# VectorE's small operations behind the following maximum, reciprocals taken from the sums in place, and a third tile's ranks as sums of signs by ScalarE

## The chip, the cores and the metric

The kernel runs on one core of a Trainium2 chip. The core has a matrix engine (TensorE, PE in the profile; its weight loads are PEld), VectorE (DVE), ScalarE (ACT), GpSimd (POOL), SyncE (SP, which here only issues DMAs), and DMA queues. The engines run their own instruction streams and meet through semaphores. The metric is device time of one execution in microseconds. An operation on an engine starts before the one ahead of it has fully ended, so in a timeline two durations overlap a little; the distance from start to start is what an operation costs its engine, and it is given where it matters.

## The reference

Two blocks, one behind the other.

```python
# attention: B, H, S, D = 8, 8, 576, 64
scores = q @ k^T / sqrt(D)
kth    = 32nd largest score of each row
attn   = softmax(where(scores >= kth, scores, -1e9))   # sum + 1e-9 in the divisor
x      = (attn @ v) as (B, S, H*D = 512)
# mixture of depths, for each batch
gate   = x @ w_gate                                    # 576 numbers
idx    = the 128 rows with the largest gate
out    = x;  out[idx] += sigmoid(gate[idx]) * (relu(x[idx] @ w1) @ w2)
```

Every one of 8 x 8 x 576 rows needs its 32nd largest score, and each batch needs the ranks of its 576 gates.

## The kernel before, in words

**Units.** A tile is 128 query rows of a batch; a batch has five tiles t = 0 to 4 (the last one, J, has 64 rows). A unit is one tile for two heads (for the last tile, four heads packed into 128 rows), so a batch has 18 units and the kernel 144. The loop `for n in range(-1, N)` (line 1192) is a software pipeline, written out by hand: the helper class `InOrder` (line 38) keeps each engine's instructions in program order, and since it records every operation, all of them carry line 46 in the profile. Nothing is planned by costs; the order in the code is the order on each engine.

**One step n of the pipeline.**

- VectorE does `bound_of(n)` (line 1143, `find_bound` at line 544): seven MAX8 over parts of each of two score rows (14 in all, `cand<-sc`), then rounds of MAX8 and MATCH_REPLACE8 on the candidates, which end in `bound`, a bound near the row's 24th largest score. After that `kth_of(n - 2)` takes two MAX8 over 584 elements (`next<-y`), whose eighth value is the wanted 32nd largest score of unit n - 2.
- ScalarE takes the exponentials of unit n - 4 (`pT`, `last`), the signs of scores against the bound of unit n - 1 with their sum (`sides`, `seen`), one mask of unit n - 3 (`less`), copies of transposed keys or queries (`kT`, `qT`), the scores of unit n + 1 out of PSUM (`sc`), and the weighted values (`xs`).
- GpSimd makes the other mask of unit n - 3 (`less`, line 603), then whatever is queued in `vector_late` for it and in `pool_late`, then `y = sc * sides` for both rows of unit n - 1 and a small fill of eight columns (`weigh_signs`, line 1160).
- TensorE turns (transposes) and masks unit n - 4, multiplies scores of unit n + 1, and multiplies by the values.

**Lists of delayed work.** `late` and `copies_late` are run by ScalarE just ahead of the next `sc` copy, `vector_late` by VectorE between the two halves of the 14 maxima (line 552), `amid_late` among the second seven, `pool_late` by GpSimd at line 1308, `kept` right behind the values, and `after_kth` behind `kth_of`.

**The end of a tile.** When a tile's last values are in `xs` (128 x 8 x 65, of which the 65th column is the sum of the weights), `keep_sums` (line 735) copies the eight sums to `sums` on ScalarE, adding 1e-9. In the next step `normalise` (line 730) takes their reciprocal on VectorE (`rden`) and multiplies on GpSimd (`x<-xs,rden`). One step later, `gates` runs `dot` (line 1028) on VectorE: the product of `x` and `wg` with its sum, the operation `prod<-x,wg`, which reads two tensors from SBUF.

**The mixture of a batch** (line 786) is a generator which the loop advances at the steps in `mix_at` (line 1072) while the next batch's units run. Its first pieces find ranks: for tiles 0 and 1, `weigh_gates` (line 839) lets ScalarE sum the signs of the differences of one gate and all gates, writing the signs themselves over the tile `pick`; for tiles 2, 3 and 4, `choose` (line 861) lets VectorE count larger gates (`junk<-gate_row,gate`, 576 elements, and an accumulator read). `choose_slot` (line 823) then compares the rank with slot numbers on GpSimd (`pick`). It is queued for both tiles 0 and 1 behind the signs of tile 1. With the usual `mix_at`, the sign of tile 0 runs at unit 8 of a batch's 18, and the two picks of tiles 0 and 1 at unit 10. Later, `add_up` (line 895) makes `place`, `row_i` and `g` on VectorE, one behind the other; `squash` (line 906) adds 1 to `g` and inverts it; `keep_least` (line 1174) reduces the 36 values of a batch's last `next`.

Of the kernel before, what the change touches and what calls it, by code (L numbers as in the profile page):

```python
# [10 lines left out]
AF = mybir.ActivationFunctionType  # L11
# [17 lines left out]
FEWEST = 0.5  # L29
# [3 lines left out]
J = 4  # L33
# [16 lines left out]
def kernel(  # L50
# [91 lines left out]
    seen = const.tile([P, NS], FP32, name="seen")  # L142
    least = const.tile([P, B], FP32, name="least")
    bounded = const.tile([P, NS], FP32, name="bounded")
    sums = const.tile([P, B * NT, H], FP32, name="sums")
    nc.gpsimd.memset(sums, 1.0)

    MIDDLE = S - 2 * (TOP_K - 8) + 1
    steps_i = const.tile([P, 2, 8], I32, name="steps_i")
# [8 lines left out]
    nc.gpsimd.memset(ranks, 0.0)  # L158


    signs = const.tile([P, B - 1, 2], FP32, name="signs")
    places = const.tile([P, B, 7], FP32, name="places")
    nc.gpsimd.memset(places, 1.0)
    slot_signs = const.tile([P, CAP], FP32, name="slot_signs")
# [59 lines left out]

    kept, values_bank = [], [None]

    after_kth = []

    def flush_copies():
        while copies_late:  # L230
# [14 lines left out]

    def flush_all():
        flush_vector()
        flush()
        flush_pool()

# [293 lines left out]
    def find_bound(sc, bound):  # L544

        cand = wkpool.tile([P, 2, 8 * PARTS], FP32, name="cand")
        best = [stats.tile([P, 2, 8], FP32, name=f"best{r}") for r in range(2)]
        best.append(bound)
        for i in range(2):

            if i == 1:
                flush_vector()
            for u in range(PARTS):
                if i == 1 and amid_late and u == amid_late[0][0]:
                    amid_late.pop()[1]()
                dve.max(
                    cand[:, i, 8 * u : 8 * u + 8],
                    sc[:, i, u * S // PARTS : (u + 1) * S // PARTS],
                )


        parts = cand.rearrange("p i (u e) -> p i u e", u=PARTS)
# [151 lines left out]
    def keep_values_of_two(t, g, av, xs):  # L714
# [7 lines left out]
        for i, (h, r) in enumerate(heads_of(t, g)[0]):  # L722
# [4 lines left out]
                in_=both[r : r + n, :].rearrange("p (g c) -> p g c", g=2),  # L727
            )

    def normalise(b, t, xs):  # L730
        n = R if t == J else P
        den = sums[0:n, b * NT + t, :]
        divide(n, xs, of_batch[b][0][0:n, t, :], den)

    def keep_sums(n, xs, den):
        act.activation(den, xs[0:n, :, D], AF.Copy, bias=1e-9)

    def divide(n, xs, x, den):
        rden = stats.tile([P, H], FP32, name="rden")
        dve.reciprocal(out=rden[0:n, :], in_=den)  # L740
        pool.tensor_tensor(
            x.rearrange("p (h d) -> p h d", h=H),
            xs[0:n, :, 0:D],
            rden[0:n, :].unsqueeze(2).to_broadcast([n, H, D]),
            ALU.mult,
        )

# [38 lines left out]
    def mixture(row0, pg, rank, exact=False, sign_sum=None):  # L786
# [47 lines left out]
        for t in range(NT):  # L834
            yield
            n = R if t == J else P


            def weigh_gates(t=t):
                total = sign_sum[:, t : t + 1]  # L840
                act.activation(
                    pick.rearrange("p t c -> p (t c)")[:, 0:S],
                    gate_row,
                    AF.Sign,
                    bias=gate[:, t : t + 1],
                    scale=-1.0,
                    accum_out=total,
                )
                if t == 1:
                    for u in range(2):  # L850
                        pool_late.append(
                            lambda u=u: choose_slot(
                                u, P, slot_signs, sign_sum[:, u : u + 1]
                            )
                        )

            if t < 2 and not exact:
                late.append(weigh_gates)
                continue

# [33 lines left out]

        def add_up():
            add_parts(place, found)
            keep_rows(
                place,
                row_i,
                row0 if isinstance(row0, float) else row0[:, 0:1],  # L900
                float(done * S - 1),
            )
            dve.tensor_scalar_max(out=g, in0=place[:, 1:2], scalar1=-88.0)
            late.append(lambda: act.activation(g, g, AF.Exp, scale=-1.0))

        def squash():
            dve.tensor_scalar_add(out=g, in0=g, scalar1=1.0)
            dve.reciprocal(out=g, in_=g)

        kept.append(lambda: after_kth.append(add_up))  # L910
        if exact:
            for todo in (kept, after_kth):
                while todo:
                    todo.pop(0)()
        yield
# [258 lines left out]
    def keep_least(b, bound, kth):  # L1174
        at = 2 * per_batch * b
        late.append(
            lambda: act.copy(
                out=bounded[:, at : at + 2 * per_batch].rearrange("p (n i) -> p n i", i=2),
                in_=bound,
            )  # L1180
        )
        dve.tensor_reduce(
            out=least[:, b : b + 1], in_=kth, axis=mybir.AxisListType.XY, op=ALU.min
        )

    def mask_of(n, on=None):
# [5 lines left out]
    for n in range(-1, N):  # L1192
# [89 lines left out]
        if is_unit(n - 4):  # L1282
            b4, t4, g4 = units[n - 4]
            values(t4, g4, pT, last, av, qkv[b4][2], 2 * DE * second)
            if n in place_steps:
                values_bank[0] = av
                next(mixtures[place_steps[n]])
                pieces[place_steps[n]] += 1
            if g4 == 0:
                xs = xpool.tile([P, H, DE], FP32, name="xs")  # L1290
                if t4 == 0:
                    x = xpool.tile([P, NT, HD], FP32, name="x")
                    pg = gates_of[b4 % 2]
                    of_batch[b4] = x, pg
            if second:
                keep_values_of_two(t4, g4 - 1, av, xs)
            if g4 == groups(t4) - 1:
                inverting = b4, t4, xs
                n4 = R if t4 == J else P
                keep_sums(n4, xs, sums[0:n4, b4 * NT + t4, :])  # L1300
            while kept:
                kept.pop(0)()

# [64 lines left out]
        b, t, g = units[m]  # L1368
        keep_values(t, g, weighed[m][3], xs)

    def sums_of(t, xs):
        n = R if t == J else P
        keep_sums(n, xs, sums[0:n, (B - 1) * NT + t, :])
# [76 lines left out]
    dve.tensor_tensor(  # L1450
        x[0:R, J, :].rearrange("p (h d) -> p h d", h=H),
        xs[0:R, :, 0:D],
        rden[0:R, :].unsqueeze(2).to_broadcast([R, H, D]),
        ALU.mult,
    )
    store_last(last_out, x)
# [77 lines left out]
        )  # L1534

    keep_least(B - 1, bounds.pop(B - 1)[:, :, :, 7], next8s.pop(B - 1)[:, :, :, 7])
    flush()
    low = modpool.tile([P, S], I32, name="low", tag="scratch")[:, 0:NS]
    dve.tensor_scalar(
# [9 lines left out]
    for what, op, than, limit in (  # L1549
# [5 lines left out]
        (sums.rearrange("p t h -> p (t h)"), ALU.min, ALU.is_gt, FEWEST),  # L1555
        (sums.rearrange("p t h -> p (t h)"), ALU.max, ALU.is_lt, MOST),
        (places[:, :, 6], ALU.min, ALU.is_gt, 0.5),
        (places[:, :, 6], ALU.max, ALU.is_lt, 1.5),
    ):
# [68 lines left out]
    def general_weights(sc):  # L1628

        p = wkpool.tile([P, 2, S], FP32, name="p", tag="y")  # L1630
        for i in range(2):
# [10 lines left out]
            e = wkpool.tile([P, S], FP32, name="e", tag="sides")  # L1642
            nc.scalar.activation(
                e, sc[:, i, :], AF.Exp, bias=shift, scale=scale
            )
# [10 lines left out]
    def general(b, row0):  # L1656
# [11 lines left out]
        for t in range(NT):  # L1668
# [14 lines left out]
            den = stats.tile([P, H], FP32, name="den", bufs=1)  # L1683
            keep_sums(rows, xs, den[0:rows, :])
            divide(rows, xs, x[0:rows, t, :], den[0:rows, :])
# [46 lines left out]
```

## Time and profile before

| what | value |
|---|---|
| median of 3 runs | 787.77 us (785.72 to 788.05) |
| the profiled execution's own time | 788.09 us |
| its span on the core | 785.8 us |
| VectorE busy, whole span | 755.1 us (96%) |
| ScalarE busy | 731.7 us (93%) |
| TensorE matmul busy | 725.5 us (92%) |
| GpSimd busy | 693.7 us (88%) |
| VectorE busy from 40 to 740 us | 699.20 of 700 us |
| ScalarE busy from 40 to 740 us | 688.49 of 700 us |

The span is the time on the core that the profile covers; what lies around it is 788.09 - 785.8 = 2.3 us. A row of the profile's groups gives engine, operation, what is written and read with shapes, the count, busy time and mean duration of one, then the idle time of the engine ahead of these operations and what ended it. A row of a timeline gives the start in us from the span's start, the duration in us, engine, line, operation, and in brackets idle time ahead of it.

### The profile page before, as it was taken

To read this page: it belongs to the slowest core of one execution; us is meant where nothing else is said; L and a number is where in the kernel's file an instruction comes from. 1 tells how busy PE (TensorE), PEld (TensorE's weight loads), DVE (VectorE), ACT (ScalarE), POOL (GpSimd) and SP (SyncE) were. 2 spreads that over 40 slices of the span, in tenths; PEclk is the share of its full clock that TensorE was granted. 3 is DMA by queue.
4 is the path that set the end of the run, shared out by engine and by line. 5 is a ranking of instruction groups with operands and counts; after the bars stand their busy time and mean duration, and the time that the engine had idled before them with its cause. 6 is when DMAs were issued, how large, how long until landed. Compare 5 with 4: busy or idle time off the path is not lost. (4 is left out here: it accounts for less than half of the span.)

```text
span 785.8 us, 33176 instructions
## 1 busy us (share of the span) xinstructions
PE 725.5 (92%) x12535; PEld 550.6 (70%) x12535; DVE 755.1 (96%) x4602; ACT 731.7 (93%) x1535; POOL 693.7 (88%) x732
## 2 busy tenths in 40 slices
PE   8888888788999989999999999999899999999987
PEld 6666666566786668766787667866687668757756
DVE  6999999999999999999999999999999999999952
ACT  5999999999999999999999999999999999989830
POOL 3899999999999999999999999999999999899821
PEclk9999999999999999999999999999999999999999
DMA  9941214121151223321232221412234102101021
GB/s 171 297 86 35 58 62 104 36 56 30 62 113 25 52 66 76 83 55 37 77 89 52 56 43 62 105 30 56 43 89 92 30 15 70 25 15 17 3 75 31
DMA packets 121751, 50.69 MB, mean 65 GB/s; under 512 B 116016, under 2 KB 116016, under 8 KB 120560
## 3 DMA queue, kind: packets, MB, share of 16 engines
q1 hardware_dynamic: 118368, 43.94, 22.9%
q0 software_dynamic: 1744, 4.20, 3.0%
q8 instruction: 101, 1.65, 0.9%
q14 instruction: 66, 0.54, 0.3%
q10 hardware_dynamic: 1472, 0.36, 0.2%
HBM read 36.93 MB, written 11.55 MB: 62 GB/s over the span
## 5 line engine op out<-in xcount | busy, mean ns | idle before, releaser
L46 POOL TENSOR_TENSOR y<-sc,sides 128x576 f32<-128x576 f32 x288 | 350.5, 1240 | 27.9 <-ACT sides L46 26.2
L46 DVE MAX8 cand<-sc 128x8 f32<-128x82 f32 (+1 forms) x2016 | 312.8, 228 | 4.6 <-ACT sc L46 4.6
L46 POOL TENSOR_SCALAR less<-sc,next 128x576 bf16<-128x576 f32 x135 | 233.7, 1731 | 24.6 <-DVE next L46 21.9
L46 ACT ACTIVATE sides<-sc,bound 128x576 fp8e4<-128x576 f32 x288 | 230.9, 802 | 2.1 <-DVE bound L46 1.5
L46 PEld LDWEIGHTS av<-v,pT 128*64 128x64 f32 x4608 | 146.9, 138 | 87.5 <-ACT last L46 79.0
L46 DVE MAX8 next<-y 128x8 f32<-128x584 f32 x288 | 204.4, 751 | 0.0
L46 PE MATMUL av<-v,pT 128*64 128x65 f32 x4608 | 166.9, 225 | 35.2 <-ACT last L46 34.9
L46 PE MATMUL ps<-kT,qT 64*128 64x288 f32 (+1 forms) x1248 | 170.4, 422 | 3.2 <-ACT sc L46 2.5
L46 PEld LDWEIGHTS <-less 64*128 64x128 bf16 (+1 forms) x2448 | 160.6, 131 | 11.2 <-POOL less L46 8.3
L46 ACT COPY sc<-ps 128x1152 f32<-128x1152 f32 x140 | 160.7, 1148 | 0.0
L46 PE MATMUL ptr<-ident,sc 64*128 64x64 f32 x2272 | 160.1, 252 | 0.0
L46 ACT ACTIVATE pT<-ptr 128x1024 f32<-128x1024 f32 x142 | 147.4, 1038 | 9.4 <-PE ptr L46 8.7
L46 PEld LDWEIGHTS ptr<-ident,sc 64*128 64x128 f32 x2272 | 137.6, 137 | 23.8 <-issue 23.6
L46 PE MATMUL ptr<-out_of_reach,less 64*128 64x64 bf16 x2272 | 147.1, 189 | 5.6 <-POOL less L46 4.9
L46 ACT ACTIVATE less<-sc,next 128x576 bf16<-128x576 f32 x147 | 115.5, 790 | 0.0
L46 PEld LDWEIGHTS ps<-kT,qT 64*128 64x128 f32 (+1 forms) x1248 | 92.6, 176 | 22.8 <-ACT sc L46 5.6
L46 DVE MATCH_REPLACE8 cand<-best,cand 128x21 f32<-128x21 f32 (+1 forms) x576 | 99.0, 180 | 0.0
L46 DVE MAX8 best<-cand 128x8 f32<-128x21 f32 (+1 forms) x576 | 90.6, 190 | 0.0
L46 ACT ACTIVATION_READ_ACCUMULATOR sides<-sc,bound 128x1 f32 x288 | 63.8, 222 | 0.0
L46 PE MATMUL h_ps<-xeT,w 128*128 128x128 f32 x464 | 61.9, 278 | 0.0
L46 PEld LDWEIGHTS av<-ident,sc 128*128 128x128 f32 x144 | 20.0, 139 | 55.9 <-issue 40.9
L46 PE MATMUL av<-vpair,last 128*64 128x130 f32 x576 | 56.9, 276 | 0.0
(167 smaller groups left out, 919.0 us busy)
## 6 DMA issues: line engine op xcount, KB each, us to landing
v<-in_v_dram SPq DMA_DIRECT2D x64, 128.0 KB, 4.0
out_dram<-x SPq DMA_DIRECT2D x8, 1024.0 KB, 3.9
rows<-in_k_dram SPq DMA_DIRECT2D x56, 128.0 KB, 3.0
rows<-in_q_dram SPq DMA_DIRECT2D x56, 128.0 KB, 3.0
w<-in_moe_w_dram SPq DMA_DIRECT2D x2, 2048.0 KB
gate_row<-row_dram SPq DMA_DIRECT2D x7, 288.0 KB, 4.4
last<-in_q_dram SPq DMA_DIRECT2D x8, 128.0 KB, 3.4
vpair<-in_v_dram SPq DMA_DIRECT2D x16, 64.0 KB, 5.1
```

Of the source, the lines that this page charges most:

```text
L46: return lambda *a, **kw: self._tc.keep_in_program_order(fn(*a, **kw))
```

## The change

Four edits.

1. A new list `after_max`, emptied by `flush_small` behind each of the 14 maxima of `find_bound`. The reduction of `keep_least`, the operations of `add_up` behind `place` (now `use_place`), and the reciprocal of `squash` go into it.
2. `keep_sums` is gone. `invert` takes the reciprocal from the column of `xs` itself and keeps it in `shares`, from which GpSimd multiplies; `rden` and the addition of 1e-9 are gone. The final checks look at `shares` instead of `sums`.
3. The ranks of tile 2 come from `weigh_gates` on ScalarE as well (`SIGNED = 3`), and not from `choose` on VectorE.
4. The signs go to a tile of their own (`gate_signs`, fp8) and no longer over `pick`, and each tile's `choose_slot` is queued right behind its signs, so the pick of tile 0 now runs at unit 8 and no longer at unit 10.

The fallback for uncertain inputs (`general`) is changed in the same way and isn't run with these inputs.

```diff
-    sums = const.tile([P, B * NT, H], FP32, name="sums")
-    nc.gpsimd.memset(sums, 1.0)
+    shares = const.tile([P, B * NT, H], FP32, name="shares")
+    nc.gpsimd.memset(shares, 1.0)
...
-    signs = const.tile([P, B - 1, 2], FP32, name="signs")
+    SIGNED = 3
+    signs = const.tile([P, B - 1, SIGNED], FP32, name="signs")
...
-    after_kth = []
+    after_kth, after_max = [], []
+
+    def flush_small():
+        while after_max:
+            after_max.pop(0)()
...
                     sc[:, i, u * S // PARTS : (u + 1) * S // PARTS],
                 )
+                flush_small()
...
+    def share_of(b, t):
+        return shares[0 : R if t == J else P, b * NT + t, :]
+
     def normalise(b, t, xs):
         n = R if t == J else P
-        den = sums[0:n, b * NT + t, :]
-        divide(n, xs, of_batch[b][0][0:n, t, :], den)
-
-    def keep_sums(n, xs, den):
-        act.activation(den, xs[0:n, :, D], AF.Copy, bias=1e-9)
-
-    def divide(n, xs, x, den):
-        rden = stats.tile([P, H], FP32, name="rden")
-        dve.reciprocal(out=rden[0:n, :], in_=den)
+        invert(xs[0:n, :, D], share_of(b, t))
+        divide(n, xs, of_batch[b][0][0:n, t, :], share_of(b, t))
+
+    def invert(den, share):
+        dve.reciprocal(out=share, in_=den)
+
+    def divide(n, xs, x, share):
         pool.tensor_tensor(
             x.rearrange("p (h d) -> p h d", h=H),
             xs[0:n, :, 0:D],
-            rden[0:n, :].unsqueeze(2).to_broadcast([n, H, D]),
+            share.unsqueeze(2).to_broadcast([n, H, D]),
             ALU.mult,
         )
...
                 total = sign_sum[:, t : t + 1]
+                unread = modpool.tile([P, S], FP8, name="gate_signs")
                 act.activation(
-                    pick.rearrange("p t c -> p (t c)")[:, 0:S],
+                    unread,
                     gate_row,
                     AF.Sign,
                     bias=gate[:, t : t + 1],
                     scale=-1.0,
                     accum_out=total,
+                    saturate=False,
                 )
-                if t == 1:
-                    for u in range(2):
-                        pool_late.append(
-                            lambda u=u: choose_slot(
-                                u, P, slot_signs, sign_sum[:, u : u + 1]
-                            )
-                        )
-
-            if t < 2 and not exact:
+                pool_late.append(lambda: choose_slot(t, P, slot_signs, total))
+
+            if t < SIGNED and not exact:
                 late.append(weigh_gates)
                 continue
...
         def add_up():
             add_parts(place, found)
+            after_max.append(use_place)
+
+        def use_place():
             keep_rows(
...
         def squash():
             dve.tensor_scalar_add(out=g, in0=g, scalar1=1.0)
-            dve.reciprocal(out=g, in_=g)
+            after_max.append(lambda: dve.reciprocal(out=g, in_=g))
...
-        dve.tensor_reduce(
-            out=least[:, b : b + 1], in_=kth, axis=mybir.AxisListType.XY, op=ALU.min
+        after_max.append(
+            lambda: dve.tensor_reduce(
+                out=least[:, b : b + 1], in_=kth, axis=mybir.AxisListType.XY, op=ALU.min
+            )
         )
...
-                keep_sums(n4, xs, sums[0:n4, b4 * NT + t4, :])
...
-    sums_of(J - 1, xs)
...
-    sums_of(J, xs)
     count(J - 1, slice(0, JP), rank)
-    rden = stats.tile([P, H], FP32, name="rden")
-    dve.reciprocal(out=rden[0:R, :], in_=sums[0:R, (B - 1) * NT + J, :])
+    invert(xs[0:R, :, D], share_of(B - 1, J))
```

More of the change, by code (lines that the diff above doesn't have):

```diff
@@ L559, in find_bound @@
                 )
+                flush_small()
         parts = cand.rearrange("p i (u e) -> p i u e", u=PARTS)
@@ L907, in squash @@
             dve.tensor_scalar_add(out=g, in0=g, scalar1=1.0)
-            dve.reciprocal(out=g, in_=g)
+            after_max.append(lambda: dve.reciprocal(out=g, in_=g))
         kept.append(lambda: after_kth.append(add_up))
         if exact:
-            for todo in (kept, after_kth):
+            for todo in (kept, after_kth, after_max):
                 while todo:
@@ L1298 @@
                 inverting = b4, t4, xs
-                n4 = R if t4 == J else P
-                keep_sums(n4, xs, sums[0:n4, b4 * NT + t4, :])
             while kept:
@@ L1369, in keep_unit @@
         keep_values(t, g, weighed[m][3], xs)
-    def sums_of(t, xs):
-        n = R if t == J else P
-        keep_sums(n, xs, sums[0:n, (B - 1) * NT + t, :])
     def mask_both(m):
@@ L1452 @@
         xs[0:R, :, 0:D],
-        rden[0:R, :].unsqueeze(2).to_broadcast([R, H, D]),
+        share_of(B - 1, J).unsqueeze(2).to_broadcast([R, H, D]),
         ALU.mult,
@@ L1536 @@
     keep_least(B - 1, bounds.pop(B - 1)[:, :, :, 7], next8s.pop(B - 1)[:, :, :, 7])
+    flush_small()
     flush()
@@ L1554 @@
         (seen, ALU.min, ALU.is_gt, float(MIDDLE - 16)),
-        (sums.rearrange("p t h -> p (t h)"), ALU.min, ALU.is_gt, FEWEST),
-        (sums.rearrange("p t h -> p (t h)"), ALU.max, ALU.is_lt, MOST),
+        (shares.rearrange("p t h -> p (t h)"), ALU.max, ALU.is_lt, 1.0 / FEWEST),
+        (shares.rearrange("p t h -> p (t h)"), ALU.min, ALU.is_gt, 1.0 / MOST),
         (places[:, :, 6], ALU.min, ALU.is_gt, 0.5),
@@ L1641, in general_weights @@
             nc.vector.tensor_scalar_mul(shift, tops[0][:, 0:1], -scale)
-            e = wkpool.tile([P, S], FP32, name="e", tag="sides")
+            e = modpool.tile([P, S], FP32, name="e", tag="scratch")
             nc.scalar.activation(
@@ L1682, in general @@
             rows = R if t == J else P
-            den = stats.tile([P, H], FP32, name="den", bufs=1)
-            keep_sums(rows, xs, den[0:rows, :])
-            divide(rows, xs, x[0:rows, t, :], den[0:rows, :])
+            den = stats.tile([P, H], FP32, name="den", bufs=1)[0:rows, :]
+            act.activation(den, xs[0:rows, :, D], AF.Copy, bias=1e-9)
+            invert(den, den)
+            divide(rows, xs, x[0:rows, t, :], den)
             dot_tile(t, x, pg)
```

## The prediction

> **What bounds the kernel now.** I read the page's busy times first, then who waited for whom on VectorE, then the busy times by stretch, to see whether the 96% is an average over unlike stages.
>
> ```profile
> PE 725.5 (92%) x12535; PEld 550.6 (70%) x12535; DVE 755.1 (96%) x4602; ACT 731.7 (93%) x1535; POOL 693.7 (88%) x732
> ...
> 40.00:740.00 700.00, 654.82 (x11733) 496.70 (x11729) 699.20 (x4307) 688.49 (x1437) 658.28 (x665) 1.00 0.24 56
> 740.00:785.80 45.80, 35.99 (x384) 26.89 (x380) 23.58 (x85) 13.27 (x35) 12.39 (x18) 0.95 0.17 46
> ```
>
> The columns are length, PE, PEld, DVE, ACT, POOL, clock, DMA share, GB/s. From 40 to 740 us VectorE idles 0.8 us of 700; its waits lie at the two ends. So in the steady part a unit lasts as long as VectorE's instructions: a bare unit has 4.74 us from start to start, one with a count 5.47 us. What VectorE is spared there is gained, as long as ScalarE (688.49 of 700) and GpSimd keep their lead. The rows concerned:
>
> ```profile
> L46 DVE CUSTOM_DVE_ANT_0 prod<-x,wg 128x512 f32<-128x512 f32 x32 | 25.4, 794 | 0.1
> L46 DVE TENSOR_SCALAR_CACHE_REDUCE junk<-gate_row,gate 128x576 f32<-128x576 f32 x14 | 11.1, 793 | 0.0
> L46 ACT ACTIVATE sums<-xs 128x8 f32<-128x8 f32 x32 | 6.9, 216 | 1.0
> L46 DVE RECIPROCAL rden<-sums 128x8 f32<-128x8 f32 x32 | 5.9, 185 | 1.4 <-ACT sums L46 1.4
> ```
>
> **The skill.** The Trainium skill, "VectorE: DVE Perf Modes", section "The DRAIN you can't avoid", says that a semaphore between two VectorE operations costs nothing beyond the drain. The trace disagrees for these short ones:
>
> ```profile
> 380.42 1.42 DVE L46 MAX8 next<-y 128x8 f32<-128x584 f32 x2
> 381.88 0.22 DVE L46 TENSOR_REDUCE least<-next 128x1 f32<-128x36 f32 x1
> ...
> 366.62 0.14 DVE L46 TENSOR_REDUCE place<-places 128x2 f32<-128x6 f32 x1
> 366.80 0.15 DVE L46 TENSOR_SCALAR row_i<-place 128x1 int32<-128x1 f32 x1
> 366.87 0.14 DVE L46 TENSOR_SCALAR g<-place 128x1 f32<-128x1 f32 x1
> 366.93 1.69 DVE L46 MAX8 cand<-sc 128x8 f32<-128x82 f32 x11
> ```
>
> Operations that don't depend on each other overlap (`row_i` to `g` is 0.07 us, `g` to the maximum 0.06); a dependent one starts after the end of the one before (`place` to `row_i` 0.18; the second `next` to `least` 0.79, where it is 0.67 to an independent maximum). The same page, in that section, says that one operation in between also removes the hazard; that the order removes the wait too is my reading. Second, "SBUF — State Buffer", section "Who interferes with whom": a VectorE instruction with two SBUF inputs contends with a GpSimd instruction that reads SBUF, and the loser blocks fully. The trace agrees: `prod` has two inputs, and beside `less` on GpSimd it takes 0.60 to 0.95 us from start to start.
>
> **Part by part.**
>
> *Third count off VectorE.* Six batches have it at their unit 11: 5.47 - 4.74 = 0.73 us each, 4.38. The last one stands with two others at 688 us, where three cost 7.24 - 4.80 = 2.44, one third 0.81. Sum 5.2 us.
>
> *Waits between small operations.* `place`: 0.18 becomes about 0.08 (its duration 0.14 less the 0.07 that neighbours overlap), 7 x 0.10 = 0.7. `least`: 7 x (0.79 - 0.67) = 0.84. `g + 1` to its reciprocal: 0.17 (387.84 to 388.01) becomes about 0.07, 7 x 0.10 = 0.7. A maximum of 0.145 us in between covers each remaining wait. Sum 2.2 us; bounds 0 (the wait stays) and 2.5. `row_i` comes some 0.2 us later in the next unit, ahead of GpSimd's fetch; `g`'s exponential on ScalarE moves a step later, still units before `squash`.
>
> *ScalarE.* A third sign costs 0.66 + 0.09 us from start to start (`pick<-gate_row,gate`, 321.38 to 322.14). The `sums` copy waits for `xs`: `xs` to `pT` is 318.32 to 318.89 = 0.57 us with it, and 308.67 to 308.92 = 0.25 in a unit without. Five tiles save 5 x 0.32 = 1.6 us a batch against 0.75 added. At unit 11 the new sign delays the next `sc` by 0.75 while VectorE comes 0.73 earlier; the lead of that `sc` (its copy's end to VectorE's first maximum) is 2.1 us there and 1.2 at the narrowest, and the copies dropped earlier in the batch add some 0.7 to it. It stays positive, so I cost this at nothing; without that cover it would cost up to 0.5 us a batch.
>
> *Reciprocal from `xs`.* The same eight elements, 65 apart. Unknown in the trace; I take the same 0.10 us from start to start. Bounds: 0.02 less or 0.05 more each, -1 to +2 us in all.
>
> *Tail.* VectorE waits for `sums` at 750.31 (1.38 us) and 755.11 (1.05 us). `xs` ended at 750.03 and 754.83, so each reciprocal starts about 0.24 us earlier, and GpSimd's or VectorE's multiply behind it too; TensorE waits 0.25 us for the gate at 752.64 in between. 0.5 us; bounds 0 and 0.6.
>
> *The pick that moves to unit 8.* It is 0.57 us on GpSimd (mean 0.61) and seems free, but `prod` meets what comes behind it. A batch's unit 8 (320.00) and unit 9 (324.80):
>
> ```profile
> 322.20 1.06 POOL L46 TENSOR_TENSOR x<-xs,rden 128x512 f32<-128x512 f32 x1
> 323.20 2.41 POOL L46 TENSOR_TENSOR y<-sc,sides 128x576 f32<-128x576 f32 x2
> 325.56 0.23 POOL L46 TENSOR_TENSOR y<-steps,seen 128x16 f32<-128x16 f32 x1
> 325.75 1.73 POOL L46 TENSOR_SCALAR less<-sc,next 128x576 bf16<-128x576 f32 x1
> ...
> 326.11 0.94 DVE L46 CUSTOM_DVE_ANT_0 prod<-x,wg 128x512 f32<-128x512 f32 x1
> 326.98 0.08 DVE L46 DVE_READ_ACCUMULATOR2_ANT gate<- 128x1 f32 x1
> ```
>
> `prod` takes 0.87 here and 0.60 where `less` began over 0.65 us ahead of it. That fits `less` keeping the port for its first 0.68 us and `prod` needing 0.53 from there: 325.75 + 0.68 + 0.53 = 326.96. With the pick (GpSimd has no idle time from 316 on to take it up), `y` starts at 323.77, the fill at 326.13, `less` at 326.33, and `prod` still at 326.11. One `prod` in the trace came so:
>
> ```profile
> 696.90 1.62 DVE L46 CUSTOM_DVE_ANT_0 prod<-x,wg 128x512 f32<-128x512 f32 x1
> 697.05 0.21 POOL L46 TENSOR_TENSOR y<-steps,seen 128x16 f32<-128x16 f32 x1
> 697.24 1.72 POOL L46 TENSOR_SCALAR less<-sc,next 128x576 bf16<-128x576 f32 x1
> 698.45 0.08 DVE L46 DVE_READ_ACCUMULATOR2_ANT gate<- 128x1 f32 x1
> ```
>
> It lost to the fill and to `less`: 697.24 + 0.68 + 0.53 = 698.45, as measured. So I expect 326.33 + 1.21 = 327.54, a `prod` of 1.43 instead of 0.87 to 0.95 (mean of six 0.895): 6 x 0.54 = 3.2 us lost. The other bound: `prod` gets in before `less`, as one did at 52.42 that came deep inside a `y`; then it takes 0.60 to 0.73, 6 x 0.23 = 1.4 gained. I take the loss.
>
> At unit 13 the reverse: before, `less` is late there because GpSimd waited for ScalarE's second sign at unit 10 (0.31 us) with two picks behind it. With one pick moved away, `less` comes 0.2 us earlier against `prod`, whose 0.68 to 0.73 becomes 0.60: 0.5 us gained.
>
> **Sum.** 5.2 + 2.2 + 0.5 + 0.5 - 3.2 = 5.2 us of the profiled 788.09 (span 785.8 and 2.3 around it): 782.9. That execution is 0.3 above the median; from 787.77 I get 782.6.
>
> **Rivals.**
>
> *A, the port is won:* `prod` slips in. For it, the 52.42 case; against it, 696.90, which came nearer to the fill. 8.4 + 1.4 = 9.8 gained: 778.0.
>
> *B, ScalarE takes over:* from unit 11 VectorE waits for `sc`. It speaks for this that ScalarE is 98% busy; against, the leads above. It decides if the copies' 1.6 us is not realised because ScalarE waits for TensorE instead. At 0.4 to 0.5 us in six batches 2.7 is lost: 785.3.
>
> *C, slower:* the port again, at units 9 and 13 of six batches, if a `prod` must wait for a `y`, the fill and `less` back to back: up to 1.17 + 0.19 + 0.68 = 2.04 us. Gains without port effects are 7.9, so it decides from 0.66 us a piece over twelve; at 1.0, 12 - 7.9 = 4 slower: 792. Against it: my reckoning puts no `prod` at the start of a `y`.
>
> *D, the change doesn't do what it says:* the order doesn't shorten the waits, reciprocals cost 0.05 more and the port is lost, so 5.2 + 0.5 + 0.5 - 3.2 - 2 = 1: 786.8, no measurable change.
>
> **How the numbers follow.** Forecast 0.50 (782.6, own range 781 to 784.3), A 0.22, B 0.12, D 0.08, C 0.08. A measurement of this kernel tells 0.3%, 2.4 us, from no change, so faster means below 785.4. The forecast, A and over half of B lie there: 0.79; D and the rest of B 0.12; slower 0.09. The range runs from A to just beyond B, 777.3 to 786.
>
> **What would show it.** In the profile after: 7 fewer counts of 576 x 128 rows and 7 more signs; start to start `next` to the first maximum 0.67 everywhere; `xs` to `pT` 0.25; `sc` leads over 0.5 us behind unit 11 and no VectorE wait for `sc` in the middle; `prod` at unit 9 near 1.43 us in six batches (0.6 to 0.73 for A), at unit 13 near 0.60. The prediction is wrong if VectorE idles in the middle, or if the mean of `prod` moves otherwise.

## The result and the profile after

The changed kernel takes 780.12 us (median of 6 runs, 779.64 to 783.12); the kernel before, run beside it, 787.68 us (6 runs). The ratio is 0.9922, 95% interval 0.9904 to 0.9939: 0.8% faster, 7.6 us. The forecast was 782.6 us, with 777.3 to 786.0 as its range. The time lies inside, and below the forecast's own range of 781 to 784.3. Part of the 7.6 us may be scatter of the kernel before: its median in the three later sessions was 785.52 to 786.65. The reasons fit less well than the total, as the rest of this document shows.

First the busy times of the page, then a middle and an end stretch as they were shown of the kernel before, in the same columns.

```profile
PE 722.8 (93%) x12535; PEld 550.4 (71%) x12535; DVE 750.1 (96%) x4588; ACT 726.4 (93%) x1509; POOL 699.7 (90%) x732
```

```profile
40.00:740.00 700.00, 657.73 (x11774) 500.63 (x11772) 699.96 (x4307) 686.65 (x1421) 666.93 (x668) 1.00 0.24 56
740.00:778.20 38.20, 30.36 (x297) 22.53 (x293) 16.31 (x67) 8.30 (x23) 8.30 (x12) 0.99 0.19 55
```

VectorE is still the engine that sets the middle: it idles 0.04 us of 700. It has 14 instructions less, and 5.0 us less of busy time. The groups, with shapes kept apart (count, busy time, mean ns of one, idle time ahead):

```profile
L46 DVE CUSTOM_DVE_ANT_0 prod<-x,wg 128x512 f32<-128x512 f32 x32 | 25.8, 807 | 0.1
L46 ACT ACTIVATE gate_signs<-gate_row,gate 128x576 fp8e4<-128x576 f32 x21 | 16.5, 784 | 0.0
...
L46 DVE RECIPROCAL shares<-xs 128x8 f32<-128x8 f32 x32 | 6.0, 186 | 1.1 <-ACT xs L46 1.1
L46 DVE TENSOR_SCALAR_CACHE_REDUCE junk<-gate_row,gate 128x576 f32<-128x576 f32 x7 | 5.5, 791 | 0.0
```

Seven counts are gone and there are 21 signs, as the change says. The reciprocal of eight elements that lie 65 apart takes 186 ns, where the packed one took 185. The 32 `prod` of 128 rows have risen from 25.4 to 25.8 us, and this small sum hides large moves of both signs.

**Accounting by unit.** From each trace I took the time from VectorE's first maximum of one unit to that of the next, and compared equal units. Units that no edit touches agree within 0.02 us from kernel to kernel (all but x2, where VectorE waits in some), and most differences recur in four or six batches, so one profile of each carries them. Three parts make the span: what lies ahead of unit 1, the steady part (units 1 to 142), and the rest from unit 143 on.

| us | up to unit 1 | units 1 to 142 | rest | the 40 dots, start to start |
|---|---|---|---|---|
| before | 13.89 | 722.54 | 49.41 | 28.13 |
| after | 12.32 | 716.83 | 49.10 | 30.30 |

The first part varies between 11.8 and 14.1 us over the fourteen kernels profiled here, with no relation to what was edited, and the rest between 47.6 and 50.8. So the 1.6 us between the two profiles' beginnings can't be credited to the change. What can be is the 5.7 us of the steady part:

| where (unit within a batch of 18) | after minus before, us |
|---|---|
| unit 11 of six batches and unit 8 of the last: third count gone | -5.3 |
| units 1 and 2 (`least`), 16 and 17 (`place`, `row_i`, `g`), 3 (`squash`), and their places in the last batch | -2.7 |
| unit 9 of six batches: the dot costs 0.60 and no longer 0.87 to 0.95 | -1.7 |
| unit 13 of six batches: the dot costs 0.89 to 0.91 and no longer 0.60 to 0.73 | +1.3 |
| unit 5 of four batches: the dot costs 1.06 to 1.08 and no longer 0.64 | +1.8 |
| unit 9 of the last batch: its dot 2.29, before 1.56 | +0.7 |

These are rounded; the smaller differences left out make up the remainder. Counts and small operations came as forecast. The dots moved otherwise than forecast: those of unit 9 won where they were to lose, those of unit 13 lost where they were to win, and those of unit 5 were not in the forecast at all.

### The profile page after: what moved, and what is told of

Its sections match the earlier page's. It is cut to its first block, busy times and chain, and to the rows that moved or that the text cites. A ratio compares the mean times of both kernels' runs of the same rounds, so it can differ in the third digit from the quotient of the medians.

```text
span 778.3 us, 33155 instructions
## 1 busy us (share of the span) xinstructions
PE 722.8 (93%) x12535; PEld 550.4 (71%) x12535; DVE 750.1 (96%) x4588; ACT 726.4 (93%) x1509; POOL 699.7 (90%) x732
## 5 line engine op out<-in xcount | busy, mean ns | idle before, releaser
L46 ACT ACTIVATE sides<-sc,bound 128x576 fp8e4<-128x576 f32 x288 | 235.0, 816 | 1.3 <-DVE bound L46 1.1
L46 ACT COPY sc<-ps 128x1152 f32<-128x1152 f32 x140 | 162.9, 1163 | 0.0
L46 ACT ACTIVATE pT<-ptr 128x1024 f32<-128x1024 f32 x142 | 149.7, 1054 | 10.5 <-PE ptr L46 9.5
L46 ACT ACTIVATE less<-sc,next 128x576 bf16<-128x576 f32 x147 | 117.7, 806 | 0.0
L46 ACT ACTIVATION_READ_ACCUMULATOR sides<-sc,bound 128x1 f32 x288 | 68.1, 237 | 0.0
```

The source lines that it names most:

```text
L46: return lambda *a, **kw: self._tc.keep_in_program_order(fn(*a, **kw))
```

## The small operations in the trace

The kernel after, a stretch of VectorE's timeline around `place`, and one around `least` (start, duration, operation):

```profile
361.54 0.75 DVE L46 MAX8 next<-y 128x8 f32<-128x584 f32 x1
362.20 0.14 DVE L46 TENSOR_REDUCE place<-places 128x2 f32<-128x6 f32 x1
362.26 0.24 DVE L46 MAX8 cand<-sc 128x8 f32<-128x82 f32 x1
362.42 0.14 DVE L46 TENSOR_SCALAR row_i<-place 128x1 int32<-128x1 f32 x1
362.47 0.14 DVE L46 TENSOR_SCALAR g<-place 128x1 f32<-128x1 f32 x1
...
375.87 1.42 DVE L46 MAX8 next<-y 128x8 f32<-128x584 f32 x2
377.21 0.23 DVE L46 MAX8 cand<-sc 128x8 f32<-128x82 f32 x1
377.35 0.20 DVE L46 TENSOR_REDUCE least<-next 128x1 f32<-128x36 f32 x1
```

`place` to what follows it is 0.06 us (0.18 before), because a maximum that doesn't need it stands there; `row_i` to `g` 0.05. The pair of `next` is followed after 1.34 us (375.87 to 377.21), where 1.46 us passed before `least`. One maximum of 0.145 us in between is enough. The Trainium skill ("VectorE: DVE Perf Modes", section "The DRAIN you can't avoid") says that an operation in between removes the hazard of reading too early. The traces show what this does to the time: the wait between two dependent operations, which that section measured on copies and found free, costs 0.12 to 0.13 us at each place here and is gone with a maximum in between. Over the seven batches that is some 0.9 us at each of `least`, `place` and `g`, once what the dots of the same units changed is taken off.

## The experiments

Each kernel is set against runs of the kernel before on the same chip in the same session, whose median was 786.65 us for those named x, 786.01 for y and 785.52 for z.

| kernel | median us | ratio to before, 95% | units 1 to 142 | dots |
|---|---|---|---|---|
| x1, before, dot of one input | 780.23 | 0.9925 (0.9903 to 0.9947) | 718.11 | 23.75 |
| x2, after, dot of one input | 777.51 | 0.9885 (0.986 to 0.991) | 713.74 | 23.76 |
| x3, before with edit 4 alone, two signed tiles | 783.84 | 0.9968 (0.9955 to 0.998) | 720.60 | 26.42 |
| x4, after with the late pick | 780.33 | 0.9923 (0.99 to 0.9946) | 717.02 | 30.69 |
| y1, before with edit 1 alone | 784.70 | 0.9981 (0.9971 to 0.9992) | 721.40 | 29.79 |
| y2, before with edit 2 alone | 784.62 | 0.9986 (0.9974 to 0.9997) | 722.05 | 27.44 |
| y3, before with edit 3 alone | 785.42 | 0.9990 (0.998 to 1.0) | 721.81 | 31.72 |
| y4, after, dots of two tiles moved | 780.07 | 0.9925 (0.9908 to 0.9941) | 716.75 | 30.14 |
| z1, after without edit 2 | 784.43 | 0.9979 (0.9969 to 0.9989) | 720.85 | 32.58 |
| z2, after without edit 3 | 780.59 | 0.9936 (0.9918 to 0.9953) | 717.55 | 25.79 |
| z3, after without edit 1 | 781.66 | 0.9948 (0.9931 to 0.9965) | 718.76 | 29.43 |
| z4, after, dot of one tile moved | 779.74 | 0.9921 (0.9904 to 0.9937) | 716.63 | 30.05 |

### Is it the port? The dot with one input (x1, x2)

```diff
-        dve.tensor_tensor_reduce(
+        dve.tensor_scalar(
             out=prod[0:n, 0:HD],
             in0=x,
-            in1=wg[0:n, :],
-            scale=1.0,
-            scalar=0.0,
+            scalar1=1.0,
+            scalar2=None,
             op0=ALU.mult,
             op1=ALU.add,
             accum_out=g,
```

In these two kernels the dot sums `x` alone; the product with `w_gate` is left out, so other rows are chosen, and as many.

> The kernel before, but the dot of a tile reads one tensor only (it sums x and leaves out the product with w_gate, so gates and chosen rows are other ones; the amount of work is the same). Theory P (the shared read port makes the dots long): every dot takes the same time, about 0.65 us from start to start (a count of 576 elements takes 0.72), 40 x 0.65 = 26.1 us against 28.1 measured before, so 2.0 us faster, and the spread from 0.60 to 1.56 us is gone. Theory S (the dots wait for something else): the long dots at unit 9 stay 0.27 us longer than the others, and the time changes by +2 us.

> The changed kernel with the same one-input dot (product with w_gate left out). P: all dots about 0.65 us, 26.1 us against 30.3, so 4.2 us faster than the changed kernel, about 9.7 us faster than the kernel before and 7.7 faster than x1. S: long dots stay at units 5, 9 (last batch) and 13, and it is slower than the changed kernel by 2 us.

The group of the dots in x1:

```profile
L46 DVE TENSOR_SCALAR_CACHE_REDUCE prod<-x 128x512 f32<-128x512 f32 x32 | 21.4, 670 | 0.1
```

In both kernels 38 of the 40 dots now cost 0.59 us from start to start, wherever they stand, and the two at the very end 0.61. A two-input dot costs 0.60 us at the many places where nothing disturbs it (0.599 in twelve of the kernel before), so the second input has next to no price of its own, and what a dot costs beyond 0.6 us comes with contention for its second input. (I had expected 0.65; the size was off.) The unit differences of x1 say the same: unit 9 gives back 3.3 us, unit 13 0.6 and unit 5 0.3. The Trainium skill ("SBUF — State Buffer", section "Who interferes with whom") says that a VectorE instruction with at most one SBUF input, outside the modes that use two ports, doesn't contend with GpSimd, and this pair of runs agrees. The section calls the port an exclusive lock. The traces show that a GpSimd instruction doesn't keep it to its end: `less` lasts 1.73 us, and the `prod` that came 0.36 us into it in the kernel before was through after 0.87.

In x2 the dots fall by 6.5 us against the changed kernel, but its steady part by 3.1 only; the expectation had 4.2. VectorE's waits from 40 to 740 us in x2:

```profile
DVE cand L46 <- ACT sc L46: 1.8, 4, 0.5
```

Relieved of the port, VectorE catches up with ScalarE: from the fourth batch on it waits for `sc`, up to 0.46 us at a time, and unit 11 gains 0.17 us in three batches where it gained 0.73. That is rival B's mechanism. In the changed kernel it is still covered, by a lead of 0.43 us at the narrowest once the first units are over; but of the 6.5 us that the dots give in x2 only 3.1 arrive.

### The pick (x3, x4)

x3 is the kernel before with the signs in a tile of their own and each pick behind its own signs:

```diff
-                if t == 1:
-                    for u in range(2):
-                        pool_late.append(
-                            lambda u=u: choose_slot(
-                                u, P, slot_signs, sign_sum[:, u : u + 1]
-                            )
-                        )
+                pool_late.append(lambda: choose_slot(t, P, slot_signs, total))
```

> The kernel before with the fourth edit alone: signs in a tile of their own, the pick of tile 0 right behind its signs at unit 8, two tiles signed. The prediction's step: the dot of unit 9 loses the port to the fill and the mask behind it and takes 1.43 us, 3.2 us slower. Rival A, as the changed kernel's trace suggests: the dot starts ahead of the fill, takes 0.60 us and holds GpSimd up instead; six dots of 0.895 become 0.60, 1.8 us faster, with GpSimd's mask of unit 9 about 0.5 us later than it would be.

x4 is the changed kernel with this one edit turned round.

> The changed kernel with the pick of tile 0 back behind the signs of tile 1 (unit 10). If the early pick is what made the dot of unit 9 short, that dot is near 0.88 us again in six batches (+1.7 us); the dot of unit 13, which takes 0.90 us in the changed kernel because a y of GpSimd covers its start, then finds GpSimd at another place, and takes 0.6 to 1.0. Together -0.5 to +2.5 us against the changed kernel. The prediction's step would have it 3.7 us faster.

In x3 unit 9 costs 0.27 to 0.34 us less in each of the six batches, 1.7 us, and 0.2 us less in the last; unit 13 gives back 0.01 to 0.07 each. Rival A's outcome, then. In x4 unit 9 is back within 0.12 us of before (+1.5 us against the changed kernel), and unit 13 costs 1.2 us less than in the changed kernel. So beside the other edits the early pick wins 1.5 us at unit 9 and pays 1.2 at unit 13; the loss at unit 5 stays in x4, so it isn't the pick's.

How the dot wins is in the timeline of the kernel after, in the batch whose unit 9 was shown of before:

```profile
320.17 2.40 POOL L46 TENSOR_TENSOR y<-sc,sides 128x576 f32<-128x576 f32 x2
322.53 0.70 POOL L46 TENSOR_TENSOR y<-steps,seen 128x16 f32<-128x16 f32 x1
323.21 1.72 POOL L46 TENSOR_SCALAR less<-sc,next 128x576 bf16<-128x576 f32 x1
...
322.48 0.68 DVE L46 CUSTOM_DVE_ANT_0 prod<-x,wg 128x512 f32<-128x512 f32 x1
323.08 0.09 DVE L46 DVE_READ_ACCUMULATOR2_ANT gate<- 128x1 f32 x1
```

`prod` begins at 322.48, 0.05 us ahead of the fill of eight columns. It takes 0.60 us, and it is the fill that is held up: 0.70 us where it takes 0.22, with `less` 0.48 later. GpSimd pays. At unit 9 that costs VectorE nothing; a like delay at unit 3 does cost it at unit 5, as shown below.

### One edit alone (y1, y2, y3)

y1 has `after_max` and its three uses, y2 the reciprocal from `xs`, y3 the third sign. (y3 also has the tile `gate_signs`, since the signs of a third tile would overwrite the picks of the first two where they were.)

The line that marks y1 (and the like for `least` and `squash`), then that of y2, then that of y3:

```diff
+            after_max.append(use_place)
```

```diff
-                keep_sums(n4, xs, sums[0:n4, b4 * NT + t4, :])
```

```diff
-            if t < 2 and not exact:
+            if t < 3 and not exact:
```

> The kernel before with the first edit alone (small operations behind the following maximum). The sum over units from 1 to 142 falls by 0.13 us at each of three places in seven batches, 2.7 us (the prediction had 2.2), and the dots stay where they are (0.87 to 0.95 at unit 9, 0.68 to 0.73 at unit 13, 0.64 at unit 5). If the order didn't take the waits away, nothing changes. The start (unit 0) and the stretch behind unit 142 vary by 1 to 2 us between executions of any kernel and are read apart.

> The kernel before with the second edit alone (reciprocals from xs in place, no copies of sums). Units 1 to 142: no change within 0.3 us, since VectorE has the same operations; ScalarE has 1.6 us a batch less to do, so its lead for the next scores rises. Tail: 0.5 us less by the prediction, hidden in its scatter. If a reciprocal that reads 65 apart cost more, 38 of them would show it as longer units 2, 4, 8, 12 and 16.

> The kernel before with the third edit alone (tile 2's ranks by ScalarE; signs in a tile of their own because they'd overwrite picks otherwise; picks of tiles 0 and 1 at unit 10 as before). Counts: 0.73 us less in six units 11 and 0.85 at unit 8 of the last batch, 5.2 us. If the 1.7 us that the changed kernel loses at unit 5 comes from ScalarE running later (VectorE has moved ahead by 0.73 us a batch and ScalarE got 0.75 more), it shows here as well, and VectorE waits for scores at units 10 to 12, since the 1.6 us a batch of the copies aren't saved: 1 to 4 us faster in all. If unit 5 comes from the small operations or the sums, it is 5 us faster.

y1: the small operations give 2.8 us, about what they give in the changed kernel, but the dots, which were expected to stay, rise by 1.66 us (0.16 to 0.23 at unit 9 of four batches, 0.6 and 0.4 at units 9 and 13 of the last), so 1.1 us remain. y2: 0.5 us. The dots fall by 0.7, 0.5 of it at unit 13, and 0.2 is lost in small amounts elsewhere; the reciprocal costs 0.10 us from start to start in both. y3: the counts give 5.3 us, and 4.5 of it is given back: the dot of unit 3 costs 0.51 to 0.53 us more in four batches, that of unit 13 0.35 to 0.5 more in five, the last batch's at unit 9 0.8 more, and unit 12 0.21 to 0.25 more in four batches, where VectorE waits for `sums`; the dot of unit 9 is 1.2 us better. 0.7 us remain, and the measured time can hardly be told from no change. The expectation had asked which edit makes unit 5 dear. None does alone: its dot costs 0.60 to 0.65 us in y1, y2 and y3.

### One edit undone (z1, z2, z3)

z1 is the changed kernel with the copies of sums and `rden` back, z2 the one with the third tile counted by VectorE, z3 the one without `after_max`. The lines that mark them, in this order:

```diff
+                keep_sums(n4, xs, sums[0:n4, b4 * NT + t4, :])
```

```diff
-    SIGNED = 3
+    SIGNED = 2
```

```diff
-            after_max.append(use_place)
```

> The changed kernel with edit 2 alone undone (ScalarE copies the sums again). Theory additive: an edit is worth beside the others what it is worth alone; edit 2 alone took 0.5 us off the steady part, so 780.1 + 0.5 = 780.6 us. Theory cover: the dropped copies are what lets ScalarE carry the third sign; without them the lead of the scores over VectorE at units 11 to 13 (0.46 us in the changed kernel) is used up by about 0.3 us a tile and VectorE waits for scores at units 12 or 13, 0.2 to 0.4 us in six batches, 1.2 to 2.4 us, and the dots may shift by 1 us either way: 781.5 to 783.5 us.

> The changed kernel with edit 3 alone undone (two tiles ranked by signs, the third counted by VectorE). Theory additive: edit 3 alone took 0.73 us off the steady part, so 780.8 us. Theory masked gain: edit 3's own saving is 5.3 us of counts in the changed kernel too, and what hid it when alone was ScalarE's lateness and the port; here the counts come back in full (+5.3 at unit 11 and in the last batch) and the dots of unit 13 and unit 5, which the third sign made late, get 1 to 3 us cheaper: 782.5 to 784.5 us.

> The changed kernel with edit 1 alone undone (the small operations stand behind one another again). Theory additive: edit 1 alone took 1.14 us off, so 781.3 us. Theory port: the waits come back in full, 2.7 us at units 1, 3 and 16, and VectorE, 0.13 us later in a batch from unit 1 on, meets GpSimd less badly at unit 5, where a dot costs 1.06 us: the dots fall by 0 to 1.75 us, so 781.1 to 782.8 us. The two theories part only if unit 5 stays: then 782.8 us with dots of 30.3 us.

z2 comes out within 0.5 us of the changed kernel: the third sign is worth next to nothing, though the counts are back in full (unit 11 +4.4 us, the last batch's unit 8 +0.85). The dots make up for them: 25.79 us against 30.30, 1.8 us less at unit 13, 1.7 at unit 5 and 0.9 in the last batch's unit 9. The expectation had 1 to 3 us for that; it is 4.5. The additive theory hits the number only because edit 3 gives back as much alone (in y3, through the port and the waits for `sums`) as it does beside the others.

The timelines show why. z2 first, a batch's unit 13:

```profile
340.58 2.40 POOL L46 TENSOR_TENSOR y<-sc,sides 128x576 f32<-128x576 f32 x2
342.93 0.23 POOL L46 TENSOR_TENSOR y<-steps,seen 128x16 f32<-128x16 f32 x1
343.12 1.74 POOL L46 TENSOR_SCALAR less<-sc,next 128x576 bf16<-128x576 f32 x1
...
343.74 0.68 DVE L46 CUSTOM_DVE_ANT_0 prod<-x,wg 128x512 f32<-128x512 f32 x1
```

and the same unit of the kernel after, with GpSimd's two waits for ScalarE that lie a unit or two ahead of it:

```profile
334.34 0.61 POOL L46 TENSOR_SCALAR pick<-slot_signs,signs 128x128 bf16<-128x128 f32 x1 [0.16 <-ACT gate_signs L46]
...
336.37 1.22 POOL L46 TENSOR_TENSOR y<-sc,sides 128x576 f32<-128x576 f32 x1 [0.25 <-ACT sides L46]
...
340.43 2.40 POOL L46 TENSOR_TENSOR y<-sc,sides 128x576 f32<-128x576 f32 x2
342.79 0.67 POOL L46 TENSOR_TENSOR y<-steps,seen 128x16 f32<-128x16 f32 x1
343.44 1.72 POOL L46 TENSOR_SCALAR less<-sc,next 128x576 bf16<-128x576 f32 x1
...
342.41 0.97 DVE L46 CUSTOM_DVE_ANT_0 prod<-x,wg 128x512 f32<-128x512 f32 x1
343.31 0.08 DVE L46 DVE_READ_ACCUMULATOR2_ANT gate<- 128x1 f32 x1
```

In z2 `less` has had the port for 0.62 us when `prod` comes, and `prod` hardly notices. In the kernel after, VectorE comes 0.73 us earlier, since its count at unit 11 is gone. GpSimd had nothing taken off its work and doesn't follow; it even waits 0.41 us for the sign and for ScalarE's `sides`. Against VectorE it is 1.2 us late: the fill would come 1.98 us into unit 13 (342.79 less 340.81, where VectorE's first maximum of the unit starts) and not 0.78 (342.93 less 342.15 in z2). So `prod` falls 0.80 us into a `y`, waits inside it, costs 0.90 us, and then holds up the fill.

At unit 5 (of the same batch, 40 us earlier) `prod` meets GpSimd at another place, too. In z2, and then in the kernel after:

```profile
302.85 1.72 POOL L46 TENSOR_SCALAR less<-sc,next 128x576 bf16<-128x576 f32 x1
...
303.42 0.70 DVE L46 CUSTOM_DVE_ANT_0 prod<-x,wg 64x512 f32<-64x512 f32 x1
```

```profile
302.25 1.71 POOL L46 TENSOR_SCALAR less<-sc,next 128x576 bf16<-128x576 f32 x1
...
302.37 1.15 DVE L46 CUSTOM_DVE_ANT_0 prod<-x,wg 64x512 f32<-64x512 f32 x1
303.45 0.07 DVE L46 DVE_READ_ACCUMULATOR2_ANT gate<- 64x1 f32 x1
```

`less` leads `prod` by 0.57 us in z2 and by 0.12 after. The reckoning of the prediction, `less` + 0.68 + 0.53, gives 303.46, and 303.45 is measured.

Where the 0.45 us between the two leads comes from is seen one and two units earlier. First the kernel after, units 3 and 4, and then unit 4 of z2:

```profile
292.22 0.67 DVE L46 CUSTOM_DVE_ANT_0 prod<-x,wg 128x512 f32<-128x512 f32 x1
292.31 2.17 POOL L46 TENSOR_SCALAR less<-sc,next 128x576 bf16<-128x576 f32 x1
...
297.00 1.71 POOL L46 TENSOR_SCALAR less<-sc,next 128x576 bf16<-128x576 f32 x1
```

```profile
297.60 1.72 POOL L46 TENSOR_SCALAR less<-sc,next 128x576 bf16<-128x576 f32 x1 [0.61 <-DVE next L46]
```

In z2 GpSimd is early at unit 4 and waits 0.61 us for VectorE's `next`. In the kernel after it is late enough at unit 3 that `prod` goes ahead of `less` and holds it up: 2.17 us and not 1.71. The wait at unit 4 is gone, and GpSimd is 0.45 us later against VectorE. The four batches whose dot of unit 5 is dear are the four in which `less` was held up so at unit 3. A dot that wins the port can thus be paid for by the next one.

z1 has the copies of sums back, and takes 784.43 us: 4.0 us more in the steady part, though edit 2 alone was worth 0.5. The expectation's cover theory has the direction, but its 783.5 was too little. VectorE's waits from 40 to 700 us (total, times, longest) as the view has them, which leaves out a fifth of 0.15 us:

```profile
DVE rden L46 <- ACT sums L46: 0.6, 4, 0.2
```

By unit these waits cost more than their idle time: unit 12 +1.3 us, 0.24 to 0.27 in each of the five batches. ScalarE's lead at unit 9 and unit 12 is used up (0.03 us from the copy of `sc` to VectorE's first maximum), and ahead of unit 12 VectorE loses 0.12 us in four batches. The larger part is the dots: GpSimd is later still, and the dot of unit 9 costs 1.33 us in four batches (+3.0 us), unit 13 +0.8; unit 5 is 1.9 better. z3, without the small operations' new places, takes 781.66 us. The small operations' own 2.8 us come back, unit 5 loses its collision (-1.8), and the dot of unit 3 gets one (0.30 to 0.34 us more in four batches). It was to part the two theories only if unit 5 stayed; it didn't, so z3 decides nothing between them.

### Can the dot be put elsewhere? (y4, z4)

The number says behind how many of the second seven maxima a tile's dot comes. y4 moves tiles 1 and 4, z4 tile 4 alone:

```diff
-            amid_late.append((4 if gating[1] in (1, 2) else 2, lambda a=gating: gates(*a)))
+            amid_late.append(((2, 6, 4, 2, 6)[gating[1]], lambda a=gating: gates(*a)))
```

```diff
-            amid_late.append((4 if gating[1] in (1, 2) else 2, lambda a=gating: gates(*a)))
+            amid_late.append(((2, 4, 4, 2, 6)[gating[1]], lambda a=gating: gates(*a)))
```

> The changed kernel with the dots of tiles 1 and 4 behind four more or two more maxima (units 13 and 5: place 6 of the second seven). P: the dot at unit 5 then starts 1.88 us into the unit, behind the stretch in which the mask holds the port (1.18 to 1.86), and takes 0.62 us instead of 1.08 in four batches; the one at unit 13 starts as the y of GpSimd lets go (1.89) and takes 0.60 instead of 0.90 in six: 3.6 us faster than the changed kernel. S: no change.

> The changed kernel with the dot of the fifth tile alone moved from the third to the seventh of the second seven maxima (unit 5). Theory local: the dot at unit 5 falls from 1.06 to 0.62 us in four batches and nothing else moves: 1.7 us less, 778.4 us. Theory shifting: VectorE, spared at unit 5, comes earlier against GpSimd later in the batch and other dots (units 9 and 13) take up most of it, as when two tiles' dots were moved: 779.6 to 780.3 us.

In both the dot of unit 5 gets cheaper (1.6 us less in y4, 2.0 in z4), and nothing is won beyond the scatter: 780.07 and 779.74 us, as z4's shifting theory had it. In z4 unit 13 takes back 1.3 us and unit 9 0.3. z4, the batch whose unit 13 was shown:

```profile
342.03 2.39 POOL L46 TENSOR_TENSOR y<-sc,sides 128x576 f32<-128x576 f32 x2
344.39 0.66 POOL L46 TENSOR_TENSOR y<-steps,seen 128x16 f32<-128x16 f32 x1
...
343.67 1.31 DVE L46 CUSTOM_DVE_ANT_0 prod<-x,wg 128x512 f32<-128x512 f32 x1
```

VectorE, some 0.4 us earlier since unit 5, now meets the same `y` 0.46 us behind its start instead of 0.80, and waits longer: 1.24 us. y4, which was expected to win 3.6 us, moved the dot of unit 13 as well, but that one gives only 0.2 us; unit 3 (0.8 us in all, 0.3 of it in the last batch) and unit 9 (0.8) took it back. As I read it, GpSimd doesn't get earlier when a dot is spared, and so VectorE runs into the next thing that GpSimd is late with.

**Alone and beside the others.** The worth of each edit in the steady part, from the table above:

| us | alone (against before) | beside the others (undone in after) |
|---|---|---|
| 1, small operations | 1.1 | 1.9 |
| 2, no copies of sums | 0.5 | 4.0 |
| 3, third tile by signs | 0.7 | 0.7 |
| 4, early pick | 1.9 | 0.2 |

Alone they sum to 4.3 us, together they give 5.7. Edit 2 is worth eight times as much beside the others. The waits for `sums` and the lead that is used up in z1 suggest that it is the third sign that needs it; a kernel with edits 2 and 3 alone was not run. Only x2, which leaves work out, is faster than the changed kernel by more than the scatter.

## Why the prediction was right or wrong

**The bound: right.** VectorE idles 0.04 us from 40 to 740 us, and what it is spared in a unit comes off that unit.

**Third count, 5.2 us: right as a term, wrong as the worth of the edit.** It measures 5.3 us. But z2 shows that the edit is worth 0.7 us, because of the next point.

**ScalarE, "I cost this at nothing": this step failed.** The cover named was the lead of `sc`, and it held: no wait of VectorE for `sc` in the middle, though the lead fell to some 0.46 us at units 12 and 13, a little under the 0.5 that the prediction named. The step looked only at whether VectorE would wait. It didn't ask what GpSimd, which stands between the two and got no relief, would do when VectorE comes 0.73 us earlier and ScalarE's sign later. It came 1.2 us late against VectorE, and the dots, mainly those of units 13 and 5 and of the last batch, paid 4.5 us.

**Waits between small operations, 2.2 us: right**, 2.7 by unit in the changed kernel.

**Reciprocal from `xs`, nothing: right.** 0.10 us each, as before.

**Tail, 0.5 us: not told.** The last part is 0.3 us shorter, and it scatters by more than that. VectorE's waits for `sums` (2.4 us) have become waits for `xs` of 1.7 us in the whole profile, and that is as far as it goes.

**The pick that moves to unit 8, 3.2 us lost: this step failed.** Its times were right: the fill was put 0.02 us behind `prod`, and came 0.05 behind. The conclusion was drawn from one `prod`, that of 696.90, which lost to a fill behind it. The six dots of unit 9 won, and gained 1.7 us (x3: 1.7 alone); rival A had 1.4. The dot of 696.90 is the last batch's, and at that place it costs 1.3 to 2.4 us in every kernel here with a two-input dot: the general case was taken from the exception. Why that place differs stays open.

**Unit 13, 0.5 us gained: right without edit 3** (in z2 the dots of that tile cost 0.07 us in all beyond 0.60 us each; before, it was 0.6 us in all), **wrong with it**: 1.3 us lost. It is the same omission as in ScalarE's step.

**The sum.** It was right by compensation. For everything but the third sign the prediction's terms give 2.2 + 0.5 - 3.2, a loss of 0.5 us ahead of the tail; z2 gains 5.0. For the third sign they give 5.2; it is 0.7. The two errors, 5.5 and 4.5 us, have opposite signs and nearly cancel. So with the dots, whose mean was to be a test: the terms let the forty rise by 2.7 us together, and they rise by 2.2, but at units 13 and 5 and not at unit 9. That agreement is luck.

**The rivals.** A was right about the place and wrong about the total, since unit 13 and unit 5 took its gain. B doesn't occur in the changed kernel, but does in x2 and, by 0.12 us in four batches, in z1. C named units 9 and 13 as places where a `prod` could meet a `y`: that happens at unit 13, at 0.2 us a piece, far from the 0.66 that it needs. D is out: the order shortens the waits.

## What to carry to other kernels

When two engines share a port, the time of an instruction depends on where the other engine stands, so an edit's worth is not a property of the edit: measure it alone and undone, and expect the sums to differ. When work is taken off the engine that sets the pace, ask which engine beside it isn't relieved; that one may be late from then on, and what is timed against it moves. A case that appears once in a trace is no rule: the other dots at hand should have been reckoned by it first.

## What the runs showed of the hardware

- A `prod` that starts 0.05 us ahead of GpSimd's small `tensor_tensor` (the fill) holds it up: 0.70 us where it takes 0.22. One that starts 0.09 us ahead of `less` stretches that from 1.71 to 2.17 us. A `prod` that starts inside a `y` waits until about 1.1 us after that `y` began and mostly goes ahead of what follows: 0.80 us into it, it costs 0.90 us; 0.46 us into it, 1.24 us.
- It doesn't always go ahead. In the last batch's unit 9 of the kernel after, `prod` waits 0.87 us inside a `y` and then lets both the fill and `less` pass, 2.29 us in all:

```profile
687.73 2.39 POOL L46 TENSOR_TENSOR y<-sc,sides 128x576 f32<-128x576 f32 x2
690.07 0.22 POOL L46 TENSOR_TENSOR y<-steps,seen 128x16 f32<-128x16 f32 x1
690.27 1.73 POOL L46 TENSOR_SCALAR less<-sc,next 128x576 bf16<-128x576 f32 x1
...
689.20 2.36 DVE L46 CUSTOM_DVE_ANT_0 prod<-x,wg 128x512 f32<-128x512 f32 x1
691.49 0.08 DVE L46 DVE_READ_ACCUMULATOR2_ANT gate<- 128x1 f32 x1
```

- That `prod` ends where `less` + 0.68 + 0.53 puts it (691.48), and with one input (x2) it costs 0.59 us, so it is the port. What lets it lose here and win at unit 13 isn't its phase alone: in z4 a `prod` 1.03 us into a `y` won, in the kernel before the one at 696.90, 1.04 us into a `y`, lost. This stays open, and nothing here was run to settle it.
